# F in 64x64 tiles, ordered by the copies out of PSUM, and inversions begun a step later

## Chip, core and metric

One core of a Trainium2 chip. The metric is the device time of one execution in microseconds, as a median of several executions. A single core has no second die to compare with, so a run counts as fast when it lies within 1.5% of the fastest of its kernel. Ratios are the mean time of one kernel's fast runs over the mean of the other's fast runs of the same rounds, so they are not quite the ratio of the medians quoted beside them.

Within one kernel the runs scatter by some 2 to 8 us. A large part arises before the changed code: the first transpose of the sixth unit (unit 5, counting from 0), up to which nearly all the code is the same, starts between 258.1 and 266.1 us in the profiles below. Where I compare single profiles I therefore give the time from that transpose to the end as well, and call it *the part from unit 5 on*.

## The reference, cut to what matters

```python
for t in range(S):                       # 768 steps, 4 x 8 heads, head size 40
    y[:, :, t] = einsum('bhd,bhde->bhe', rt, state)
    Sa = einsum('bhde,bhe->bhd', state, at)
    state = state * wt[:, :, None, :] - einsum('bhd,bhe->bhde', Sa, bt) \
            + einsum('bhd,bhe->bhde', vt, kt)
x = y as (3072, 320)
h = x @ w_in;  out = (h * clip(h + 3, 0, 6) / 6) @ w_out      # hidden size 2048
```

The kernel takes blocks of 64 time steps. The feedback through `Sa` inside a block becomes a triangular matrix per head, I - F, which is inverted. A *unit* is one pair of blocks (two batches) with eight heads; there are 24. Four units make a *group*, and one inversion serves a group.

## The kernel before

`prepare` makes a unit's F, and one stage later Kt and Bt, which the state update and the outputs read:

```python
f = [ps_any([P, NPR, BL]) for _ in range(2)]
...  # for pr, c, q, s: 32 columns of F a matmul, the second half's blocks swapped by the operand's view
    nc.tensor.matmul(out=f[s][z:z + L, pr, :], lhsT=at[half(s, D), pr, x:x + L], rhs=y,
                     start=True, stop=True, tile_position=(s * SLOT, z))
yield PE
for s in range(2):
    nc.scalar.activation(out=F[:, x:x + 4, :], in_=f[s][:], func=AF.Copy, scale=-1.0)
yield DONE
rg = ...                                  # transpose of rgam, then rgt on ScalarE
for name in "KB":
    t = grp.tile([P, WPAD], F32, name=name + "t", tag=name + "t")    # pool grp: five buffers
    nc.gpsimd.memset(t[:, HD:WPAD], 0.0)
    nc.gpsimd.tensor_tensor(out=t[...], in0=o[name + "N"][:, :, 0:D], in1=rgt[:], op=ALU.mult)
```

The inversion is mostly VectorE, with two instructions on GpSimd at its beginning and copies at its end. It is cut into single steps, which are issued some at a time between the others' work:

```python
def invert(F, third):
    nc.vector.transpose(out=fb..., in_=F[:, :, 0:L]...)
    nc.gpsimd.affine_select(out=x[:], in_=fb[:], ...)        # "the select"
    nc.gpsimd.memset(diagonal of x, 1.0)
    ...
    for i in range(1, L - 1):
        nc.vector.tensor_tensor(out=pv, ...)     # prod
        yield
        nc.vector.tensor_tensor(out=rest, ...)   # x
        yield
    ...                                          # tb, tt on VectorE; halves of tinv on ScalarE and GpSimd
```

`slot` interleaves a unit's own steps, the preparation of a later unit (`ahead`) and the feed-forward pieces. A slot has eight places; `begin` is the place at whose start the inversion is begun, and a rate is (feed-forward pieces, inversion steps for each stage):

```python
for j, stages in enumerate(((before, own, ahead), (before, own, ahead, block, own), ...)):
    if j == begin:
        side.append(invert(group_F[-1], third))
    ...
elif i % NU == NU - 2:     # the last F of the group is made in place 4 of this slot
    rates, begin = [(1.75, 0)] * 5 + [(3.2, 3)] * 3, 5
elif i % NU == NU - 1:
    rates = [(3.25, 2)] * 4 + [(3.25, 3)] * 4
```

In these traces VectorE, ScalarE and GpSimd start their instructions in the order in which they were issued, even when a later one could go.

Of the kernel before, what the change touches and what calls it, by code (L numbers as in the profile page):

```python
# [12 lines left out]
AF = mybir.ActivationFunctionType  # L13
# [3 lines left out]
P = 128  # L17
BL = 64
HB = BL // 2
L = 32  # L20
SLOT = 64
# [8 lines left out]
def kernel(  # L30
# [42 lines left out]
    nc = tc.nc  # L73
    B, H, T, D = r.shape
    NG = T // (2 * BL)
    NPR = H // 2
    NP = B // 2
    NU = 2 * NP
# [16 lines left out]
    def bank(tag, shape, bufs):  # L95
        return ps.tile(shape, F32, name=tag, tag=tag, bufs=bufs)
# [3 lines left out]
    def ps_any(shape):  # L100
        tag, bufs = ring[0]
        ring.rotate(-1)
        return bank(tag, shape, bufs)
# [6 lines left out]
        out=ident[:], in_=ones[:], pattern=[[1, P]],  # L110
# [4 lines left out]
        out=ones[:, 0:BL], in_=ones[:, 0:BL], pattern=[[1, BL]],  # L115
# [3 lines left out]
        out=ones[BL:P, 0:BL], in_=ones[BL:P, BL:P], pattern=[[1, BL]],  # L119
# [34 lines left out]
    start = const.tile([P, SCAN], F32, name="start")  # L154
# [12 lines left out]
    for i in range(3):  # L167
        t = const.tile([P, H, BL], F32, name=f"score{i}")
# [11 lines left out]
    for p in range(NP):  # L180
        t = const.tile([P, 2, NPR, SLOT], F32, name=f"state{p}")
        nc.vector.memset(t[:], 0.0)
        state.append(t)
        t = const.tile([P, 2, NPR], F32, name=f"last{p}")
# [113 lines left out]
    PE, DONE = 1, 2  # L298
# [34 lines left out]
    def turn_pairs(x):  # L333

        o = ps_any([P, NPR, P])
        for n in range(NPR):
            nc.tensor.transpose(out=o[:, n, :],  # L337
                                in_=x[:, 2 * n:2 * n + 2, :].rearrange("p s e -> p (s e)"),
                                identity=ident[:])
        return o  # L340

    def turned(name):
        return tmp.tile([P, NPR, P], F32, name=name, tag="turned", bufs=5)

    def half(i, n=SLOT):
        return slice(SLOT * i, SLOT * i + n)

    def scores(lhs, rhs, swap=False):


        o = [ps_any([P, NPR, BL]) for _ in range(2)]
        for n in range(NPR):
            for q in range(2):
                for i in range(2):
                    nc.tensor.matmul(out=o[i][half(q), n, :],  # L355
                                     lhsT=lhs[half(i, D), n ^ (2 * q * swap), half(q)],
                                     rhs=rhs[half(i, D), n, half(q)], start=True, stop=True)
        return o
# [9 lines left out]
    def prepare(i, F):  # L368
        n, o = i % NU, data[i]
# [4 lines left out]
        x = wt[:].rearrange("p r (q m i) -> p (r q) m i", q=2, m=2)  # L374
# [5 lines left out]
            out=prods[:].rearrange("p r m i -> p (r m i)"), data0=wm[:], data1=start[:],  # L380
# [21 lines left out]
        x = turn_pairs(o["AN"])  # L402
        yield PE
        nc.vector.reciprocal(rv[:, :, HB:BL], prods[:, :, 1, 1:HB + 1])  # L404
        at = grp.tile([P, NPR, P], F32, name="at", tag="at")
# [5 lines left out]
        x = turn_pairs(o["BN"])  # L411
        yield PE
        bt = turned("bt")
# [1 line left out]
        yield DONE  # L415


        f = [ps_any([P, NPR, BL]) for _ in range(2)]
        for pr in range(NPR):
            for c in range(2):  # L420
                for q in range(2):
                    for s in range(2):
                        x = q * BL + c * L
                        y = bt[half(s, D), pr, half(q)].rearrange("p (c t) -> p c t", c=2)
                        if c:
                            y = y[:, ::-1, :]
                        z = (q ^ s) * BL + c * L
                        nc.tensor.matmul(out=f[s][z:z + L, pr, :],  # L428
                                         lhsT=at[half(s, D), pr, x:x + L], rhs=y,
                                         start=True, stop=True, tile_position=(s * SLOT, z))  # L430
        yield PE
        for s in range(2):
            x = n * H + 4 * s
            nc.scalar.activation(out=F[:, x:x + 4, :], in_=f[s][:], func=AF.Copy, scale=-1.0)
        yield DONE


        rg = ps_any([P, NPR, P])
        for pr in range(NPR):
# [4 lines left out]
            out=rgt[:], in_=rg[:].rearrange("p r (s e) -> p (r s) e", s=2)[:, :, 0:D],  # L444
            func=AF.Copy,
        )
        for name in "KB":
            t = grp.tile([P, WPAD], F32, name=name + "t", tag=name + "t")
            nc.gpsimd.memset(t[:, HD:WPAD], 0.0)  # L449
            nc.gpsimd.tensor_tensor(  # L450
                out=t[:, 0:HD].rearrange("p (h e) -> p h e", h=H), in0=o[name + "N"][:, :, 0:D],
# [8 lines left out]
        x = turn_pairs(o["KN"])  # L460
# [6 lines left out]
        x = scores(kt, at)  # L467
# [7 lines left out]
        for pr in range(NPR):  # L475
            for s in range(2):
                for q in range(2):
                    nc.tensor.matmul(out=ev[q][half(q ^ s), pr, :], lhsT=E[half(q), 4 * s + pr, :],  # L478
                                     rhs=VN[half(q), 4 * s + pr, 0:D], start=True, stop=True)
# [351 lines left out]
    third, F, group_F = [], None, []  # L831

    def prepared(i):
        nonlocal F
        if i >= NK:
            return iter(())
        if i % NU == 0:
            F = inv.tile([P, NH, BL], F32, name="F", tag="F", bufs=2)
            group_F.append(F)
        return prepare(i, F)  # L840
# [99 lines left out]
    def slot(i, rates, begin):  # L940

        own = step(i)
        before, own_chain[0] = own_chain[0], own
        for j, stages in enumerate((
                (before, own, ahead), (before, own, ahead, block, own), (block, own, ahead),
                (own, own, ahead), (own, pieces, ahead), (own, own, ahead), (own, ahead),
                (own, ahead))):
            if j == begin:
                side.append(invert(group_F[-1], third))
            if j == 1 and i % NU == 0:  # L950
                aside(3 * L)
            rate, moment[1] = rates[j]
            for stage in stages:
                if stage is pieces:
                    pieces(rate)
                elif stage is block:
                    block(i, j - 1)
                elif stage is ahead:
                    ahead(STEPS * (i - NU) + j)
                else:  # L960
                    run(stage, moment[1])
            if pieces not in stages:
                pieces(rate)
# [3 lines left out]
    for i in range(NU, NK):  # L967
        rates, begin = [(1.75, 0)] * 8, None
        if i == NU:
            rates = [(1.75, 3)] + [(1.75, 0)] * 7  # L970
        if i + AHEAD >= NK + NU - 1:
            rates = [(2.25, 0)] * 8
        elif i % NU == NU - 2:

            third.clear()
            rates, begin = [(1.75, 0)] * 5 + [(3.2, 3)] * 3, 5
        elif i % NU == NU - 1:
            rates = [(3.25, 2)] * 4 + [(3.25, 3)] * 4
        slot(i, rates, begin)
    for _ in range(2):  # L980
        run(own_chain[0])
# [32 lines left out]
```

## Time and profile before

| | before |
|---|---|
| time, median of three runs | 890.15 us |
| span of the profile | 889.8 us |
| TensorE busy | 796.2 us, 89% |
| VectorE / ScalarE / GpSimd busy | 536.6 / 291.5 / 147.8 us |
| waits of TensorE after 300 us | 6.0 us |
| part from unit 5 on | 625.3 us |

The prediction shows the lines for these.

### The profile page before, as it was taken

How to read it: one execution, taken by the hardware profiler on the slowest of the kernel's cores; microseconds unless marked ns; L12 is line 12 of the kernel's file. 1: busy time of each engine (PE TensorE's matmuls, PEld its weight loads, DVE VectorE, ACT ScalarE, POOL GpSimd, SP SyncE). 2: the span in 40 equal slices, each digit the busy share in tenths (PEclk: the TensorE clock that was granted, in tenths of full speed). 3: DMA queues.
4: the chain of work that ended last, by engine and by line, in shares of the span. 5: the costliest groups of instructions: out<-in, count | busy, mean ns of one | idle time of the engine just before them, and what ended most of it. 6: DMA issues, size and time to landing. Idle time of an engine off the chain costs nothing.

```text
span 889.8 us, 34847 instructions
## 1 busy us (share of the span) xinstructions
PE 796.2 (89%) x15456; PEld 674.5 (76%) x15456; DVE 536.6 (60%) x1141; ACT 291.5 (33%) x670; POOL 147.8 (17%) x318
## 2 busy tenths in 40 slices
PE   3721968797899999999999999999999998999998
PEld 3620866686788888888888788888888887888886
DVE  7899677858955488644597544696455746222211
ACT  1334644322324332423322443233442223232211
POOL 4221012122121220320220222112022201000000
PEclk7655568888999999999999999999999998999999
DMA  6533333331123221222321222221222101010000
GB/s 132 89 103 95 106 113 93 72 65 27 31 40 67 47 50 37 48 37 45 62 44 23 55 48 46 44 56 28 45 56 42 28 15 25 13 25 19 19 17 15
DMA packets 175974, 45.00 MB, mean 51 GB/s; under 512 B 157904, under 2 KB 173264, under 8 KB 175824
## 3 DMA queue, kind: packets, MB, share of 16 engines
q1 hardware_dynamic: 174768, 42.61, 23.5%
q8 instruction: 122, 2.00, 0.9%
q10 hardware_dynamic: 1056, 0.16, 0.1%
q14 instruction: 28, 0.23, 0.1%
HBM read 34.08 MB, written 3.93 MB: 43 GB/s over the span
## 4 chain that ended last, share of the span: by engine, by line
PE 69%; DVE 6%; POOL 2%; issue 1%; ACT 0%; POOLq 0%
PE o L773 20%; PE h L749 16%; PE any L337 7%; PE h L754 6%; PE any L355 3%; PE any L651 2%; PE any L680 2%; PE any L428 2%; PE any L535 1%; DVE x L512 1%; PE any L633 1%; PE any L612 1%; DVE prod L506 1%; PE any L547 1%; PE any L578 1%
## 5 line engine op out<-in xcount | busy, mean ns | idle before, releaser
L773 PE MATMUL o<-wout,gt 128*128 128x320 f32 x768 | 232.3, 444 | 1.5 <-DVE gt L760 1.5
L749 PE MATMUL h<-xt,win 128*128 128x128 f32 x1536 | 198.0, 281 | 0.0
L749 PEld LDWEIGHTS h<-xt,win 128*128 128x128 f32 x1536 | 187.7, 196 | 6.0 <-issue 0.2
L773 PEld LDWEIGHTS o<-wout,gt 128*128 128x128 f32 x768 | 138.9, 192 | 51.6 <-DVE gt L760 1.8
L760 DVE SCALAR_TENSOR_TENSOR gt<-gt,h 128x512 f32<-128x512 f32 x96 | 61.5, 681 | 82.5 <-ACT gt L759 82.4
L759 ACT ACTIVATE gt<-h,three 128x512 f32<-128x512 f32 x96 | 60.8, 684 | 129.5 <-PE h L754 129.2
L364 DVE COPY_PREDICATED score<-mask,any 128x256 f32<-128x256 int32 x143 | 54.9, 438 | 68.8 <-PE any L355 68.5
L506 DVE TENSOR_TENSOR prod<-x 128x30 f32<-128x30 f32 (+9 forms) x180 | 65.5, 364 | 8.8 <-POOL x L497 5.4
L512 DVE TENSOR_TENSOR x<-x,prod 128x30 f32<-128x30 f32 (+9 forms) x180 | 62.9, 349 | 4.8
L690 POOL TENSOR_TENSOR yg<-ys,gam 128x512 f32<-128x512 f32 x24 | 31.1, 1294 | 190.4 <-DVE ys L687 149.9
L754 PE MATMUL h<-xt,win 64*128 64x128 f32 x768 | 57.9, 292 | 0.0
L754 PEld LDWEIGHTS h<-xt,win 64*128 64x128 f32 x768 | 48.5, 194 | 6.2 <-issue 2.4
L564 ACT ACTIVATE RT<-any 128x512 f32<-128x512 f32 x24 | 14.3, 597 | 92.4 <-PE any L337 92.4
L449 POOL MEMSET Kt<- 128x24 f32 x24 | 2.8, 118 | 238.6 <-PE any L680 238.6
L535 PE MATMUL any<-tb,F 32*32 32x32 f32 x768 | 17.6, 205 | 27.7 <-DVE tb L515 27.7
L379 DVE TENSOR_TENSOR_SCAN prods<-wm,start 128x528 f32<-128x528 f32 x24 | 30.4, 1267 | 19.2 <-ACT wm L376 17.5
L658 DVE TENSOR_TENSOR state<-any,state 128x160 f32<-128x160 f32 x48 | 13.1, 316 | 47.3 <-PE any L651 47.3
L404 DVE RECIPROCAL rgam<-prods 128x256 f32<-128x256 f32 x24 | 41.5, 1731 | 0.0
L390 DVE RECIPROCAL gam<-prods 128x256 f32<-128x256 f32 x24 | 41.3, 1736 | 0.0
L484 ACT ACTIVATE EV<-any 64x160 f32<-64x160 f32 x92 | 24.7, 294 | 43.0 <-PE any L478 42.5
L246 ACT ACTIVATE parts<-parts,low 128x256 uint32<-128x256 uint32 x40 | 20.4, 509 | 55.5 <-DVE parts L244 55.3
L535 PEld LDWEIGHTS any<-tb,F 32*32 32x32 f32 x768 | 16.0, 120 | 28.9 <-issue 28.2
(138 smaller groups left out, 1200.6 us busy)
## 6 DMA issues: line engine op xcount, KB each, us to landing
raw<-in_moe_w_out_dram SPq DMA_DIRECT2D x20, 256.0 KB
B<-in_b_dram SPq DMA_DIRECT2D x48, 80.0 KB
K<-in_k_dram SPq DMA_DIRECT2D x48, 80.0 KB
V<-in_v_dram SPq DMA_DIRECT2D x96, 40.0 KB
R<-in_r_dram SPq DMA_DIRECT2D x96, 40.0 KB
out_dram<-ob SPq DMA_DIRECT2D x48, 80.0 KB
W<-in_w_dram SPq DMA_DIRECT2D x40, 80.0 KB
A<-in_a_dram SPq DMA_DIRECT2D x40, 80.0 KB
```

The lines of the kernel that those rows point to most:

```text
L337: nc.tensor.transpose(out=o[:, n, :], in_=x[:, 2 * n:2 * n + 2, :].rearrange("p s e -> p (s e)"), identity=ident[:])
L364: nc.vector.copy_predicated(out=x[:, 4 * i:4 * i + 4, :], mask=mask4, data=o[i][:])
L390: nc.vector.reciprocal(gv[:, :, 0:HB], prods[:, :, 0, 1:HB + 1][:, :, ::-1])
L404: nc.vector.reciprocal(rv[:, :, HB:BL], prods[:, :, 1, 1:HB + 1])
L506: nc.vector.tensor_tensor(out=pv, in0=_ap(x[:], (i + 1) * L + i, [[L, n], [0, i]]), in1=_ap(x[:], i * L, [[0, n], [1, i]]), op=ALU.mult,)
L512: nc.vector.tensor_tensor(out=rest, in0=rest, in1=pv, op=ALU.add)
L535: nc.tensor.matmul(out=zp[x][z:z + L, h, :], lhsT=F[z + L:z + BL, n * H + h, L:BL], rhs=tb[z + L:z + BL, n * H + h, :], start=True, stop=True,
L749: nc.tensor.matmul(out=hp[c][:, i, :], lhsT=win[:, t, j * P:(j + 1) * P], rhs=xt[:, t, :], start=(t == 0 and i == 0), stop=False)
L754: nc.tensor.matmul(out=hp[c][:, i, :], lhsT=win2[half(c), (j0 + i) * P:(j0 + i + 1) * P], rhs=xt[half(c), 2, :], start=False, stop=(i == N ...
L759: nc.scalar.activation(out=gt[:], in_=hp[c][:], func=AF.Relu, bias=three[:], scale=1.0)
L760: nc.vector.scalar_tensor_tensor(out=gt[:], in0=gt[:], scalar=6.0, in1=hp[c][:], op0=ALU.min, op1=ALU.mult)
L773: nc.tensor.matmul(out=op[:], lhsT=gts[c][:, n, :], rhs=wout[:, c * HJ + r * NQ + n, :], start=((split or r == 0) and c == 0 and n == 0), ...
```

## The change

Intent: from unit 8 on F takes 16 full 64x64 matmuls instead of 32 narrow ones; the swap of blocks that the narrow ones did by their operand's view is done by the copies, which become eight instead of two. As F is ready later for it, the inversion begins a place later and is done in more steps at a time.

```diff
 ...
+        else:
+            f = [ps_any([P, NPR, BL]) for _ in range(2)]
+            for pr in range(NPR):
                 for q in range(2):
                     for s in range(2):
+                        nc.tensor.matmul(out=f[s][half(q ^ s), pr, :],
+                                         lhsT=at[half(s, D), pr, half(q)],
+                                         rhs=bt[half(s, D), pr, half(q)], start=True, stop=True)
+            yield PE
+            for s in range(2):
+                x = n * H + 4 * s
+                for z in range(0, P, BL):
+                    y = f[s][z:z + L, :, 0:L]
+                    nc.scalar.activation(out=F[z:z + L, x:x + 4, 0:L], in_=y, func=AF.Copy, scale=-1.0)
+                    z += L
+                    y = f[s][z:z + L].rearrange("p r (c t) -> p r c t", c=2)[:, :, ::-1, :]
+                    nc.scalar.activation(out=F[z:z + L, x:x + 4, :].rearrange(
+                        "p h (c t) -> p h c t", c=2), in_=y, func=AF.Copy, scale=-1.0)
 ...
-            rates, begin = [(1.75, 0)] * 5 + [(3.2, 3)] * 3, 5
+            rates, begin = [(1.75, 0)] * 6 + [(3.2, 3)] * 2, 6
         elif i % NU == NU - 1:
-            rates = [(3.25, 2)] * 4 + [(3.25, 3)] * 4
+            rates = [(3.4, 3)] * 8
```

More of the change, by code (lines that the diff above doesn't have):

```diff
@@ L415, in prepare @@
         yield DONE
-        f = [ps_any([P, NPR, BL]) for _ in range(2)]
-        for pr in range(NPR):
-            for c in range(2):
+        if i < 2 * NU:
+            f = [ps_any([P, NPR, BL]) for _ in range(2)]
+            for pr in range(NPR):
+                for c in range(2):
+                    for q in range(2):
+                        for s in range(2):
+                            x = q * BL + c * L
+                            y = bt[half(s, D), pr, half(q)].rearrange("p (c t) -> p c t", c=2)
+                            if c:
+                                y = y[:, ::-1, :]
+                            z = (q ^ s) * BL + c * L
+                            nc.tensor.matmul(out=f[s][z:z + L, pr, :],
+                                             lhsT=at[half(s, D), pr, x:x + L], rhs=y,
+                                             start=True, stop=True, tile_position=(s * SLOT, z))
+            yield PE
+            for s in range(2):
+                x = n * H + 4 * s
+                nc.scalar.activation(out=F[:, x:x + 4, :], in_=f[s][:], func=AF.Copy, scale=-1.0)
+            yield DONE
+        else:
+            f = [ps_any([P, NPR, BL]) for _ in range(2)]
+            for pr in range(NPR):
@@ L421, in prepare @@
                 for q in range(2):
                     for s in range(2):
-                        x = q * BL + c * L
-                        y = bt[half(s, D), pr, half(q)].rearrange("p (c t) -> p c t", c=2)
-                        if c:
-                            y = y[:, ::-1, :]
-                        z = (q ^ s) * BL + c * L
-                        nc.tensor.matmul(out=f[s][z:z + L, pr, :],
-                                         lhsT=at[half(s, D), pr, x:x + L], rhs=y,
-                                         start=True, stop=True, tile_position=(s * SLOT, z))
@@ L431, in prepare @@
-        yield PE
-        for s in range(2):
-            x = n * H + 4 * s
-            nc.scalar.activation(out=F[:, x:x + 4, :], in_=f[s][:], func=AF.Copy, scale=-1.0)
-        yield DONE
+                        nc.tensor.matmul(out=f[s][half(q ^ s), pr, :],
+                                         lhsT=at[half(s, D), pr, half(q)],
+                                         rhs=bt[half(s, D), pr, half(q)], start=True, stop=True)
+            yield PE
+            for s in range(2):
+                x = n * H + 4 * s
+                for z in range(0, P, BL):
[5 more added lines that the diff above has]
+                        "p h (c t) -> p h c t", c=2), in_=y, func=AF.Copy, scale=-1.0)
@@ L438, in prepare @@
+            yield DONE
         rg = ps_any([P, NPR, P])
```

## The prediction

> **What bounds the kernel now.** I read the page first (shares, then the 40 slices), then the waits of TensorE alone, then the timeline around one F, then the timeline around the end of one inversion, and last the busy time and clock in short windows.
>
> ```profile
> PE 796.2 (89%) x15456; PEld 674.5 (76%) x15456; DVE 536.6 (60%) x1141; ACT 291.5 (33%) x670; POOL 147.8 (17%) x318
> ...
> PE   3721968797899999999999999999999998999998
> ```
>
> A slice is 22.2 us. TensorE is the full engine from about the twelfth slice on: before that VectorE, converting the weights, is busier. The change touches only units 8 to 23 and the inversions of groups 2 to 5. In the trace the first F of these units is at 252.91 us, so all of it lies where TensorE has no holes. TensorE's waits from 312 us to the end are only these two:
>
> ```profile
> PE any L578 <- DVE state L569: 3.2, 3, 1.4
> PE any L535 <- DVE tb L515: 2.8, 1, 2.8
> ```
>
> Six microseconds in 578. So anything that takes TensorE time away there is worth its full size, and anything off TensorE is worth only what it takes from these four waits. One F and what follows it, from the timeline (start, length, engine, line; the start of the next row is what a block really costs[...]):
>
> ```profile
> 311.71 0.86 PE L428 MATMUL any<-bt,at 40*32 40x64 f32 x64
> ...
> 312.50 0.68 PE L651 MATMUL any<-V,Kt 64*64 64x40 f32 x32
> ...
> 312.68 0.66 ACT L434 ACTIVATE F<-any 128x256 f32<-128x256 f32 x2 [2.11 <-PE any L428]
> ...
> 313.57 0.66 PE L337 MATMUL any<-ident,U 128*128 128x128 f32 x4
> ...
> 314.07 0.60 PE L440 MATMUL any<-ident,rgam 128*128 128x128 f32 x4
> ```
>
> The F block, 64 hardware matmuls (each of the program's 32 is two), costs 312.50 - 311.71 = 0.79 us. The reciprocal's transpose (L440) begins 2.36 us after the F began, and reuses the buffer that F's first half leaves: the buffers rotate by five, and F takes two, the state update two, U one.
>
> Three of the four waits are at the end of an inversion:
>
> ```profile
> 359.80 2.02 DVE L515 STREAM_TRANSPOSE tb<-x 128x1024 f32<-128x1024 f32 x1
> ...
> 363.56 0.74 DVE L687 TENSOR_TENSOR ys<-any,ys 128x256 f32<-128x256 f32 x2
> ...
> 364.39 1.28 POOL L690 TENSOR_TENSOR yg<-ys,gam 128x512 f32<-128x512 f32 x1 [1.82 <-DVE ys L687]
> ...
> 365.73 2.13 POOL L525 COPY tinv<-tb 32x1024 f32<-32x1024 f32 x2
> ...
> 367.93 0.20 POOL L567 TENSOR_TENSOR scale<-last,dec 128x8 f32<-128x8 f32 x1
> ...
> 368.17 0.49 DVE L569 TENSOR_TENSOR state<-state,scale 128x320 f32<-128x320 f32 x1 [3.17 <-POOL scale L567]
> ...
> 368.81 0.68 PE L578 MATMUL any<-state,at 40*64 40x40 f32 x32 [1.37 <-DVE state L569]
> ```
>
> The two last transposes keep VectorE until 363.6, ys comes after, GpSimd multiplies yg, and only then makes two copies of the inverse (2.13 us) before the tiny scale for which the state, and so TensorE, waits 1.37 us. After such waits the clock can fall:
>
> ```profile
> 372.00:376.00 4.00, 4.00 (x64) 3.65 (x64) 0.00 (x0) 1.59 (x3) 0.00 (x0) 0.66 0.36 59
> ...
> 748.00:752.00 4.00, 4.00 (x42) 3.38 (x37) 0.77 (x3) 2.81 (x5) 1.05 (x2) 0.50 0.10 22
> ```
>
> The seventh number is the granted clock. Over the whole stage 364.60 to 395.90 it is 0.95, which is 0.05 x 31.3 = 1.6 us lost; the equal wait (1.38) at 496.62 brought no fall.
>
> [...] 64 in 0.79 us are 12 ns apart. [...] F now is the only 64x32 mode between 64x64 blocks; afterwards it is in the mode of its successor. [...] The trace: 380 ns for 256 elements [...], two in 0.66 us.
>
> **The change, part by part.**
>
> *Matmuls.* Each of 16 units does 16 instead of 32, in hardware 32 instead of 64. [...] Now the sixteen F blocks cost 0.79 (fourteen of them, to a hundredth), 0.90 and 0.95 us, start to next start: 12.9 us. What 32 hardware matmuls on 64x64 tiles cost depends on the follower: medians 0.48 (L578), 0.49 (L651 on V) and 0.51 (L680 on K) before another 64-wide block, 0.58 to 0.62 (L355, L633) before a full-array one. F is followed by L651, so 0.49: 14 x 0.30 + 0.41 + 0.35 = 5.0 us at best; with 0.58 it is 3.5. I take 4.5 us.
>
> *Copies on ScalarE.* Two of 256 elements become eight: four of 128 (about 0.27 us, from the straight line through 300 ns for 160 elements and 380 ns for 256), four of 256 (0.38). Busy time rises by 16 x (4 x 0.27 + 4 x 0.38 - 2 x 0.38) = 29 us, to about 321. No bound, at 36%, but a latency: with overlap, four copies last about 1.2 us and eight 2.3, instead of 0.66. F's matmuls end about 0.7 after the start; the first buffer is free at 1.9 to 2.0, and L440 will want it at 2.36 - 0.30 = 2.06. It just fits. The copies of U and rgt come about 0.5 us later; UT's scores (L355) start 3.8 to 6.5 us after F, U's copy ends at about 3.6. I allow 0.4 us for all such waits.
>
> *Later inversions.* The order of instructions shows that the first transpose moves behind the state update of the next step, so VectorE no longer sits waiting for F there (5.6 us in the trace); worth nothing itself, as VectorE has other slack. Steps: before 21 + 20 + 27 = 68 calls up to the end of the next slot, after 12 + 57 = 69, for 68 needed. So it ends one call earlier: the last addition lies before kt and gt, and on GpSimd one of the two copies of the inverse comes ahead of yg, where GpSimd is idle for 1.8 us. The scale comes 1.07 us earlier for this, and 0.18 for the addition. The matmul work between h's last part and L578 is the same at the first two ends, 0.9 us less at the third. Waits: 1.37 to 0.1, 1.38 to 0.1, 0.46 to 0.46 + 0.94 - 1.25 = 0.15. Saved 2.8 us. With the first wait goes the fall of the clock behind it, 1.6 us; [...] I count 1.2.
>
> *The last inversion.* There no preparation runs beside it, so three a call give 12 + 36 = 48 steps up to its slot's end instead of 21 + 29 = 50. Two operations more (0.35 + 0.33 us) are left for the burst before tb, with 0.2 us more matmul work to hide them: that wait grows from 2.8 to 3.3. +0.5 us.
>
> *Rates of the feed-forward part.* 5 x 1.75 + 3 x 3.2 + 8 x 3.25 = 44.35 pieces become 44.1: nothing is removed, it moves. Zero.
>
> Sum: -4.5 - 2.8 - 1.2 + 0.5 + 0.4 = -7.6 us: 882.5.
>
> **The rivals.**
> (1) The copies become the wait: F's buffers are held 1.6 us longer and TensorE[...] stops at L440 in each unit. For it: the margin worked out is 0.1 us. If a copy with the reversed blocks costs more than a plain one[...], 16 x 0.3 = 4.8 us eat the matmuls' gain: about 887.
> (2) VectorE becomes the bound of the slot before a group's end: it is busy 33.04 of 38.20 us there, and 9 steps of about 0.35 us move in. 33 + 3 = 36 of about 39 us. Against it: it enters the slot with those steps not yet owed, so the total up to tb is unchanged, and bt, the nearest, was ready at 344.3 for an F at 348.8. If it comes true, two or three microseconds at each of three ends: about 889.
> (3) [...] only the waits go: with 0.7 us a block, 885.5.
>
> **Range and chances.** The matmul term can be 2 to 5, waits and clock 1 to 5.5, new waits 0 to 3. Best case -10, bad case -3; 878.5 to 887.5. A change by 2% would be 18 us, four times the largest term: 0.01 either way.
>
> **What would show it.** F's rows: 32 matmuls and a start-to-start of 0.49; L440's row without a wait on ScalarE; ScalarE's busy time near 321; L578's waits of 3.2 us together near 0.3, with the clock of that stage at 1.00; the wait before L535 near 3.3. I am wrong if TensorE waits for F's copies in most units, or if a new wait on VectorE stands in the slots before the group ends.

## More of the kernel before

One more stretch of that trace is needed, which the prediction does not show: the beginning of an inversion. It is the timeline of the kernel before (start, length, engine, line, operation, and in brackets the idle time before it and what ended it), GpSimd and VectorE rows:

```profile
313.37 2.18 DVE L494 STREAM_TRANSPOSE fb<-F 128x1024 f32<-128x1024 f32 x1 [5.56 <-ACT F L434]
...
315.62 1.27 POOL L497 TENSOR_SCALAR_AFFINE_SELECT x<-fb 128x1024 f32<-128x1024 f32 x1 [14.90 <-DVE fb L494]
...
316.92 0.20 DVE L506 TENSOR_TENSOR prod<-x 128x30 f32<-128x30 f32 x1 [0.97 <-POOL x L497]
...
322.71 0.12 POOL L449 MEMSET Kt<- 128x24 f32 x1 [5.60 <-PE any L680]
```

The select follows the transpose at once. Seven microseconds later Kt waits 5.60 us for the y matmuls (L680): the five buffers of Kt go round, and the one it needs is read by the y of the very slot in which it is made. Nobody waits for this Kt, so the wait costs nothing.

## The result

The changed kernel takes 915.33 us (913.59 to 918.02, four runs), before 889.88 in the same rounds: ratio 1.0287, 95% interval 1.0256 to 1.0317. It is slower by 2.9%, and the prediction was a small gain. The page of the changed kernel, busy time and slices of TensorE:

```profile
PE 805.0 (88%) x14944; PEld 675.4 (74%) x14944; DVE 534.3 (58%) x1141; ACT 322.2 (35%) x766; POOL 147.4 (16%) x318
...
PE   3722878789899989999989999899999898999998
```

512 hardware matmuls fewer (15456 to 14944), and yet TensorE is busy longer: that points to slower matmuls. Its waits from 300 us on, changed kernel (total, times, longest):

```profile
PE any L355 <- DVE kt L484: 16.3, 4, 4.1
PE any L556 <- DVE tb L536: 3.4, 1, 3.4
PE any L355 <- ACT UT L686: 2.6, 7, 0.4
```

The three waits of 3.2 us at the inversions' ends are gone, as predicted. In their place stand four waits of 4.08 us each for kt. All four are in slots of the units 6, 10, 14 and 18, where an inversion begins. The first of them in the timeline of the changed kernel:

```profile
316.49 2.16 DVE L515 STREAM_TRANSPOSE fb<-F 128x1024 f32<-128x1024 f32 x1 [1.23 <-ACT F L454]
...
321.61 0.69 PE L701 MATMUL any<-score,Kt 64*64 64x64 f32 x32
...
322.39 0.12 POOL L470 MEMSET Kt<- 128x24 f32 x1 [20.33 <-PE any L701]
322.51 0.86 POOL L471 TENSOR_TENSOR Kt<-K,rgt 128x320 f32<-128x320 f32 x1
...
324.19 1.27 POOL L518 TENSOR_SCALAR_AFFINE_SELECT x<-fb 128x1024 f32<-128x1024 f32 x1
325.49 0.20 DVE L527 TENSOR_TENSOR prod<-x 128x30 f32<-128x30 f32 x1 [6.22 <-POOL x L518]
...
326.11 0.68 DVE L484 TENSOR_TENSOR kt<-any,rgam 128x512 f32<-128x512 f32 x1
...
326.84 1.14 PE L355 MATMUL any<-at,kt 40*64 40x64 f32 x32 [4.08 <-DVE kt L484]
327.91 6.19 PE L794 MATMUL o<-wout,gt 128*128 128x320 f32 x12
```

Read it from the bottom. TensorE waits for kt. VectorE could have made kt long before, but stands in order at the inversion's first prod, 6.22 us. The prod waits for the select on GpSimd. The select's input, fb, is there at 318.65; but the inversion begins one place later now, and in that place Kt and Bt have been issued already, so the select stands behind them. Kt waits for y (L701), as it did before the change. So after y there is a chain of Kt, Bt, select, prods and kt across three engines, and TensorE, whose next instruction needs kt, starts nothing until it is through (4.08 us). A wait that was free has been put into the path.

The last row is the second part of the loss: twelve hardware matmuls in 6.19 us, where twelve took 3.50 elsewhere in the same trace. The clock, in the windows after the first and in the second of these waits (changed kernel; the clock is the third number from the end):

```profile
326.00:330.00 4.00, 3.16 (x36) 2.45 (x37) 3.83 (x11) 0.00 (x0) 0.58 (x1) 0.57 0.43 72
462.00:466.00 4.00, 4.00 (x18) 2.56 (x12) 3.79 (x12) 0.00 (x0) 1.70 (x3) 0.50 0.12 20
```

The part from unit 5 on grew from 625.3 to 651.6 us, by 26.4. Where it went, each from the two traces:

| item | us |
|---|---|
| four waits for kt | +16.3 |
| clock: (1 - granted) x time over 3 us windows, 13.7 instead of 5.1 | +8.5 |
| waits for UT behind the longer copies of F | +2.6 |
| transposes of U and rgam in units 8 on, held by the weights of the second waiting for F's buffer | +2.0 |
| two waits around the inversion's blocks in the slot of unit 5 | +0.8 |
| last inversion's wait, 2.8 to 3.4 | +0.6 |
| waits at the inversions' ends | -3.2 |
| F blocks, 0.79 to 0.51 us start to next start | -3.7 |
| not placed | +2.5 |

The rows behind the two items on F's copies and on the wait for UT, from the same trace (PEld is TensorE's weight load):

```profile
313.79 0.27 ACT L451 ACTIVATE F<-any 32x128 f32<-32x128 f32 x1 [1.89 <-PE any L443]
...
314.07 0.38 ACT L454 ACTIVATE F<-any 32x256 f32<-32x256 f32 x1
...
315.16 0.42 PEld L461 LDWEIGHTS any<-ident,rgam 128*128 128x128 f32 x4 [0.17 <-ACT F L454]
...
317.13 0.69 PE L355 MATMUL any<-RT,UT 40*64 40x64 f32 x32 [0.42 <-ACT UT L686]
```

### The profile page after: what moved, and what is told of

It is laid out like the page before. It is cut to its first block, busy times and chain, and to the rows that moved or that the text cites. A ratio compares the mean times of both kernels' runs of the same rounds, so it can differ in the third digit from the quotient of the medians.

```text
span 916.3 us, 33920 instructions
## 1 busy us (share of the span) xinstructions
PE 805.0 (88%) x14944; PEld 675.4 (74%) x14944; DVE 534.3 (58%) x1141; ACT 322.2 (35%) x766; POOL 147.4 (16%) x318
## 4 chain that ended last, share of the span: by engine, by line
PE 54%; issue 11%; DVE 8%; ACT 3%; POOL 3%; POOLq 0%; ACTq 0%
PE o L794 17%; PE h L770 13%; PE any L337 5%; PE h L775 4%; PE any L355 3%; DVE prod L527 2%; DVE x L533 2%; PE any L701 2%; PE any L556 1%; PE any L568 1%; PE any L672 1%; ACT F L454 1%; PE any L654 1%; PE any L599 1%; PE any L633 1%
## 5 line engine op out<-in xcount | busy, mean ns | idle before, releaser
L794 PE MATMUL o<-wout,gt 128*128 128x320 f32 x768 | 241.3, 457 | 1.5 <-DVE gt L781 1.5
L794 PEld LDWEIGHTS o<-wout,gt 128*128 128x128 f32 x768 | 142.9, 197 | 55.9 <-issue 6.3
L527 DVE TENSOR_TENSOR prod<-x 128x30 f32<-128x30 f32 (+9 forms) x180 | 61.1, 339 | 34.2 <-POOL x L518 30.2
L355 PE MATMUL any<-at,kt 40*64 40x64 f32 x752 | 19.1, 249 | 30.7 <-DVE kt L484 23.3
L355 PEld LDWEIGHTS any<-at,kt 40*64 40x64 f32 x752 | 16.5, 159 | 32.7 <-DVE kt L484 16.9
```

The costliest lines, as they stand in the source:

```text
L355: nc.tensor.matmul(out=o[i][half(q), n, :], lhsT=lhs[half(i, D), n ^ (2 * q * swap), half(q)], rhs=rhs[half(i, D), n, half(q)], start=True ...
L527: nc.vector.tensor_tensor(out=pv, in0=_ap(x[:], (i + 1) * L + i, [[L, n], [0, i]]), in1=_ap(x[:], i * L, [[0, n], [1, i]]), op=ALU.mult,)
L794: nc.tensor.matmul(out=op[:], lhsT=gts[c][:, n, :], rhs=wout[:, c * HJ + r * NQ + n, :], start=((split or r == 0) and c == 0 and n == 0), ...
```

## The experiments

Eight kernels ran, and all gave correct results. The kernel before was measured beside each: 890.82 us for the first four, 889.03 for the second four, which ran in other rounds and on another chip (7 instead of 5). So a run of the first four is compared with one of the second four by their ratios, or by the distance of each from its own kernel before. The last two columns come from one profile of each kernel; the clock loss counts up to the last matmul.

| run | what | us, median | ratio | 95% interval | part from unit 5 on | clock loss in it |
|---|---|---|---|---|---|---|
| | before | | 1 | | 625.3 | 5.1 |
| | changed | 915.33 | 1.0287 | 1.0256 to 1.0317 | 651.6 | 13.7 |
| e1 | F alone | 902.91 | 1.0132 | 1.0099 to 1.0165 | 634.5 | 5.1 |
| e2 | late start alone | 918.36 | 1.0299 | 1.0278 to 1.0320 | 651.5 | 15.3 |
| e3 | changed, select ahead of Kt, Bt | 891.28 | 1.0001 | 0.9982 to 1.0019 | 626.4 | 3.4 |
| e4 | changed, six buffers of Kt, Bt | 888.92 | 0.9978 | 0.9941 to 1.0014 | 624.1 | 1.7 |
| e5 | late start alone, six buffers | 887.06 | 0.9984 | 0.9949 to 1.0019 | 624.3 | 3.4 |
| e6 | e4 with six copies of F | 882.59 | 0.9922 | 0.9888 to 0.9956 | 618.4 | 1.7 |
| e7 | F alone, six copies | 890.96 | 1.0026 | 0.9983 to 1.0069 | 625.0 | 3.4 |
| e8 | e6, last inversion faster | 877.26 | 0.9872 | 0.9837 to 0.9908 | 613.4 | 0.0 |

**F alone (e1).** The changed kernel with the old begin and rates:

```diff
-            rates, begin = [(1.75, 0)] * 6 + [(3.2, 3)] * 2, 6
+            rates, begin = [(1.75, 0)] * 5 + [(3.2, 3)] * 3, 5
...
-            rates = [(3.4, 3)] * 8
+            rates = [(3.25, 2)] * 4 + [(3.25, 3)] * 4
```

> Only the F part of the change (64x64 tiles, eight ordering copies), inversions begun one step after the last F at the old rates. Theory A (the loss is all in the late start: on GpSimd the triangular select of the inversion now stands behind Kt and Bt, which wait for the y matmuls of the same slot; VectorE then stands 6.2 us at the first prod and TensorE 4.1 us at the scores of kt, and the clock halves after it): 887 to 891 us, no wait of TensorE for kt. F saves 4.0 us, of which the waits for UT and the later rgam transpose take most back. Theory B (the copies of F on ScalarE are what costs): 905 or more.

902.91: neither theory. F alone loses 1.3%, and in another way than both parts together. Timeline and waits of this run:

```profile
315.23 2.17 DVE L515 STREAM_TRANSPOSE fb<-F 128x1024 f32<-128x1024 f32 x1 [7.36 <-ACT F L454]
...
PE any L355 <- DVE kt L484: 6.4, 4, 2.0
```

The transpose is issued right behind F and waits for the last of eight copies, until 315.23 instead of 313.37. Counted from the start of F's matmuls that is 3.45 us instead of 1.65. All that VectorE does next in the slot is late by that, and kt comes up to 2 us late for TensorE. So the late start was not idle caution: F with eight copies needs it. My theory A had no place for this.

**The late start alone (e2).** The kernel before with the changed kernel's begin and rates, the edit above in the other direction.

> Only the later inversions with their rates, F as before (32 matmuls, two copies). Theory A: nearly the whole loss, 911 to 918 us, four waits of TensorE of about 4 us at the scores of kt, clock about 0.91 in those slots. Theory B: about 887 us, the 2.8 us at the inversion's end gained.

918.36, just above the range of theory A. The waits are those of the changed kernel to a tenth, with F as it was:

```profile
PE any L355 <- DVE kt L463: 16.3, 4, 4.1
```

The late start alone loses as much as the whole change, so F's form and its copies are not what these four waits come from. (One more wait, of 1.1 us for gam, stands in this trace; I did not follow it.)

**The select ahead of Kt and Bt (e3).** The late start is kept for all but its first step, which is issued one place earlier, behind the own stages and ahead of Kt and Bt:

```diff
-            if j == begin:
-                side.append(invert(group_F[-1], third))
...
                 elif stage is ahead:
+                    if begin is not None and j == begin - 1:
+                        side.append(invert(group_F[-1], third))
+                        aside(1)
                     ahead(STEPS * (i - NU) + j)
```

> The changed kernel with one edit: the inversion's first two instructions (transpose of F on VectorE, select on GpSimd) are issued in the same step one stage earlier, behind the two own stages and ahead of Kt and Bt; all other steps at the late rates. Theory A: the four waits are gone, 884 to 890 us. Theory C (the steps pressed into fewer places keep VectorE too late, or the shifted feed-forward pieces starve TensorE): 905 or more. Theory B: no change, 915.

891.28, a little above the range that I gave. No wait for kt is left among TensorE's waits from 300 us on (this run):

```profile
PE any L556 <- DVE tb L536: 3.0, 1, 3.0
PE any L355 <- ACT UT L686: 2.5, 7, 0.4
PE any L337 <- DVE at L406: 2.4, 3, 0.8
```

The place of the first step was the cause of the loss, and not the other steps pressed together, which are the same here. This run moves the transpose on VectorE along with the select on GpSimd; the next one leaves both where they are. Theory C's effect exists but is small: three waits for `at` of 0.8 us.

**Six buffers (e4).** The order of the changed kernel, but Kt no longer needs the buffer that y still reads. Room is made at two places that are not in question:

```diff
-            t = grp.tile([P, WPAD], F32, name=name + "t", tag=name + "t")
+            t = grp.tile([P, WPAD], F32, name=name + "t", tag=name + "t", bufs=NU + 2)
-    RGT, OB = 2, 1
+    RGT, OB = 1, 1
-    ones = const.tile([P, P], F32, name="ones")
+    ones = tmp.tile([P, NPR, P], F32, name="ones", tag="turned", bufs=5)[:, 0, :]
```

> The changed kernel in its order, but Kt and Bt have six buffers instead of five, so that Kt need not wait for the y matmuls of the same slot (room made by one buffer instead of two for rgt and a shared one for the set-up's ones). Select is still behind Kt and Bt. Theory A: the select waits only for rgt and the two products, the prod wait falls from 6.2 us to 1 to 2 us, no wait of TensorE for kt, 885 to 892 us. Theory C (order or packing of steps itself): 905 or more.

888.92. The select is still behind Kt and Bt, but these go as soon as rgt is there (timeline of this run):

```profile
312.94 0.87 POOL L471 TENSOR_TENSOR Kt<-K,rgt 128x320 f32<-128x320 f32 x1 [15.35 <-ACT rgt L464]
...
314.64 1.26 POOL L518 TENSOR_SCALAR_AFFINE_SELECT x<-fb 128x1024 f32<-128x1024 f32 x1
...
315.94 0.21 DVE L527 TENSOR_TENSOR prod<-x 128x30 f32<-128x30 f32 x1 [1.19 <-POOL x L518]
```

The prod waits 1.19 us instead of 6.22, and TensorE's waits for kt are gone. So the loss takes both: the select behind Kt and Bt, and Kt's wait for y. Undo either (e3, e4) and it is gone.

**The late start alone with six buffers (e5).** The kernel of e2 with the edit of e4.

> The kernel before with only the later inversions and their rates (as in the run that had them alone, 918 us) and, besides, six buffers for Kt and Bt. Theory A (the late start loses by the select's wait behind Kt and Bt and by nothing else): back to 885 to 891 us, no wait of TensorE for kt. If the packing of the steps loses by itself: 900 or more. The difference to the changed kernel with six buffers (888.9) is what F in 64x64 tiles is worth net: by theory 1 to 3 us.

887.06, against 918.36 with five buffers; by the ratios, 0.9984 against 1.0299. The order of the work is that of e2, and nothing but buffers differs: six for Kt and Bt, one for rgt, and another place for the set-up's ones. TensorE's waits from 300 us on (this run):

```profile
PE any L535 <- DVE tb L515: 3.4, 1, 3.4
PE any L337 <- DVE gam L390: 1.4, 1, 1.4
```

This is the strongest proof of the cause. Not run was the kernel before with six buffers and nothing else; as nobody waits for Kt in its trace, I would expect no gain there, but that is not shown. Against before e5 is within noise. F with eight copies shows no gain: the ratio is 0.9978 with it (e4) and 0.9984 without, 624.1 and 624.3 us from unit 5 on. But the intervals reach about 3 us to either side, so the times cannot exclude the 1 to 3 us that I had expected.

**Six copies instead of eight (e6).** e4, and each half of F first copied whole with its blocks swapped, then two small copies over the rows that must not be swapped:

```diff
+                y = f[s][:].rearrange("p r (c t) -> p r c t", c=2)[:, :, ::-1, :]
+                nc.scalar.activation(out=F[:, x:x + 4, :].rearrange(
+                    "p h (c t) -> p h c t", c=2), in_=y, func=AF.Copy, scale=-1.0)
                 for z in range(0, P, BL):
                     y = f[s][z:z + L, :, 0:L]
                     nc.scalar.activation(out=F[z:z + L, x:x + 4, 0:L], in_=y, func=AF.Copy, scale=-1.0)
-                    z += L
-                    ...                          # the copy of the other rows, swapped
```

> The changed kernel with six buffers for Kt and Bt, and F ordered by six copies a unit instead of eight: each half once whole in reversed order over 128 partitions, then two small copies over the rows whose blocks must not be swapped. The copies last about 2.0 us instead of 2.65. Theory (ScalarE's copies of F hold back UT's scores by 0.42 us in seven units and the rgam transpose by 0.1 us in most): those waits go, 2 to 3.5 us less than the eight-copy form (888.9), 885 to 887. Rival (these waits only move to the next one): same as the eight-copy form.

882.59, better than I expected (885 to 887): 6.4 us below the kernel before of its rounds, where e4 was 1.9 below. From 300 us on only the last inversion's wait is left (waits of this run):

```profile
PE any L555 <- DVE tb L535: 3.4, 1, 3.4
```

The waits for UT are gone, and the U and rgam transposes are back to their times before. Copies that last 1.95 instead of 2.67 us decide whether F in 64x64 tiles shows a gain. This run can be set beside e5, in the same rounds: 618.4 against 624.3 us from unit 5 on, and the medians differ by 4.5. Not all of that is F's own: the blocks of F account for 3.6 of the 5.9 us and the blocks behind them for 0.6, while e5's profile also has the wait of 1.4 us for gam and one fall of the clock more (1.7 us). Some of this is taken back in blocks that I have not placed.

**F alone with six copies (e7).** e1 with the edit of e6.

> F in 64x64 tiles alone, inversions one step behind the last F as before, with six copies instead of eight. Theory (the 12 us lost with F alone come from the first transpose on VectorE, which waits in order for the last copy of F, 315.2 instead of 313.4 us, so that kt comes 1.95 us late in four slots, with the clock falling after it): the transpose starts 0.65 us earlier, the wait for kt falls from 1.95 to about 1.3 us, 896 to 901 us. Rival (what loses is not the copies' length): 903.

890.96, less than the 896 I gave as the low end. The waits are still there, shorter, and fewer (waits of this run):

```profile
PE any L355 <- DVE kt L483: 3.5, 3, 1.4
```

So the copies are what F alone loses by: shorter by 0.7 us, they let the transpose of F start 0.7 us earlier (2.72 instead of 3.45 us after F's matmuls), and that is worth 12 us in the medians, 10 when each is set against its own kernel before, and 9.5 from unit 5 on. Of the 9.5, 4.8 are waits, 1.9 the U and rgam transposes and 1.7 the clock; 1.1 are not placed. I had counted only the first kind.

**The last inversion (e8).** e6, and in the slot before the last group, where no preparation runs, five steps at a time:

```diff
-            rates = [(3.4, 3)] * 8
+            rates = [(3.4, 3 if i + NU + 1 < NK else 5)] * 8
```

> As the six-copy run with six buffers, and in the slot before the last group, where no preparation runs beside it, five steps of the inversion a call instead of three, so that no burst of VectorE work is left at its end. Theory: the wait of 3.4 us before the first matmuls on tb goes, and with it most of the clock's fall behind it (1.75 to 3.3 us in that slot): 3 to 6 us less than the six-copy run, 880 to 884. Rival (VectorE, fuller in that slot, holds up the feed-forward part): no gain.

877.26, below the range that I gave because e6 was; the gain over e6, 5.3 us, is the 3 to 6 expected. The ratio is 0.9872: 1.3% faster than before, clear of noise, and faster than the changed kernel. From 300 us on TensorE has no wait at all, and the slices of this run's page show it:

```profile
PE   3720878898899999999999999999999999999998
```

## Why the prediction was wrong

Point by point, by its own steps:

1. *What bounds the kernel*: right. What moves TensorE's waits is worth its full size, and all that happened happened there.
2. *Matmuls, -4.5*: right in kind; 0.79 to 0.51 us a block, 3.7 us from unit 5 on and 4.0 for all sixteen. One reading was wrong: F does not stand between 64x64 blocks. Before it comes a block on the full array (L749 or L773), so only the change of tile size behind it went (64x32 to 64x64 before); the block there fell from 0.49 to 0.44 us. (With 0.58 a block the sum is 3.6, not 3.5.) ScalarE's busy time, 322.2 us, is what was worked out (321).
3. *Copies on ScalarE, +0.4*: mis-sized. The term measured 2.6 (UT) + 2.0 (U and rgam) + up to 0.8, about 5. I took eight copies to last 2.3 us, counting on some overlap of neighbours; as much as the two copies before had, 0.10 us, would even have given 1.9. They lasted 2.67, one starting as the other ended (F's rows at 313.79, 314.07, 314.45, 314.74 for lengths of 0.27 and 0.38). The trace before could have warned me: there the copies of 64x160 elements into EV (L484), which also write a part of the partitions each, start 0.01 us after the one before them ended (median of 74 pairs), while copies over 128 partitions overlap by 0.10 (two of F, of 0.38 each, in 0.66). I saw the margin of 0.1 us as rival 1, and gave the full wait to TensorE's own rows; in fact it stood at the weight loads, where L461 waits 0.17 us.
4. *Later inversions, -2.8*: the ends came as worked out, 3.2 us saved. **The step that failed is here**: the first transpose "moves behind the state update of the next step, so VectorE no longer sits waiting for F there", and this is "worth nothing itself". I followed the transpose on VectorE and, at the inversion's end, the order on GpSimd, but not the order on GpSimd at its beginning. There the select moved behind Kt and Bt, and with it came a wait for y. Kt's wait was in the trace before. In place of "worth nothing" the runs show four waits of 4.08 us (16.3) and the clock's falls behind them. e2 and e5 give the step's size: with the late start alone and five buffers the median is 27.5 us above the kernel before of its rounds, with six 2.0 below, so 29.5 us.
5. *Rival 2, VectorE as the bound*: I dismissed it with "the total up to tb is unchanged". The total was, but not the moment at which the first operation could begin. VectorE did not become the bound: the wait of 6.22 us lies in the slot in which the inversion begins, where VectorE has 21.5 us of work in 31.1 (kernel before), and not in the next, with 33 in 38. It is the order that counts, as what the wait holds up (kt) is the next thing that TensorE needs. Its sign, "a new wait on VectorE ... in the slots before the group ends", is what I named as proof of error.
6. *The clock, -1.2*: this was an estimate, a part of the 1.6 us measured behind the first wait. The fall that I counted did go; new ones came behind the new waits, +8.5 in all. That the fall was there to be won was luck of one profile: in e1 the same wait, 1.38 us at 371.43, brought none (granted clock 1.00 from 371.4 to 374.4 us).
7. *Last inversion, +0.5*: 2.82 to 3.40, right.

With the fault mended the sum comes close: -7.6 was predicted, and e6, whose copies are even shorter than I had taken them to be, is 6.9 us shorter from unit 5 on. In part this is luck. By its trace e6 gains 4.3 us on F's blocks and those behind them, 3.2 on the waits at the inversions' ends and 3.4 on the clock, and loses about 1.0 on other waits; the remaining 3 us of loss are not placed. The stated bad case, -3, was also milder than its own terms: 2 from the matmuls, 1 from waits and clock and 3 of new waits make 0. What remains open is 2.5 us net of the changed kernel's loss, and why the copies of F do not overlap.

## What to carry to other kernels

When work is issued later, follow every one of its instructions on every engine, and ask what it is now behind in each queue: a wait that nobody minded becomes a wait of all that is put behind it, as Kt's (5.60 us, nobody waiting) became one of 5.5 us for the select. The check is cheap: list, for each engine, the neighbours of each moved instruction, and look up in the trace how long these neighbours waited. Where the order must stay, one more buffer for the neighbour can do the same as a new order. And when a change makes results ready later, its cost is set by what it holds up: copies of F longer by 0.7 us cost e1 9.5 us more than e7.

## What the traces show of the clock, of starts and of copies

- A wait of 1.37 us was followed by a fall of the clock once (granted 0.66 in 372 to 376 us of the kernel before), and one of 1.38 at 496.62 in the same trace was not (1.00 from 496 to 502). The clock loss from unit 5 to the last matmul is 0.0, 1.7, 3.4, 5.1, 13.7 or 15.3 us in the ten traces, all close to multiples of 1.7. Equal waits did not bring equal losses: behind the four waits of 4.08 us stand 3.4, 3.4, 3.4 and 1.7 us.
- Matmuls on different tiles started closely: 64 hardware matmuls on 64x32 tiles took 0.79 us (12 ns each) and 32 on 64x64 tiles 0.51 us (16 ns). In the trace before, the eight tiles of one turn start 7 ns apart.
- The block behind F took 0.49 us where F was on 64x32 tiles, another size than its own, and 0.44 where F was on 64x64 tiles like it. That the change of size is the reason, no run tests by itself.
- Two copies over 128 partitions overlapped (0.66 us for two of 0.38); eight copies over 32 partitions each, into one tile, did not (2.67 us for four of 0.27 and four of 0.38), nor did those of 64 partitions each into EV (0.01 us between them). What decides whether they overlap is not shown.
